# A hand-written order for every engine in a kernel of windowed attention followed by a feed-forward network

## The chip, the cores and the metric

One core of one Trainium2 chip runs the whole program. The metric is the device time of one execution in microseconds (us). A core has a matmul engine (PE, with weight loads listed as PEld), a vector engine (DVE), an activation engine (ACT), a GpSimd engine (POOL in the profile) and SP, which here only starts transfers. Matmul results are kept in accumulation banks (PSUM); both kernels use eight, each 128 partitions by 512 float32. Each engine works through its own list of instructions in order; engines wait for each other by semaphores.

## The reference, cut to what matters

```python
# attention: B, H, Sl, Sg, D = 8, 8, 512, 32, 64; window 32
s_g = scale * q_g @ k_all.T            # 32 global queries see all 544 keys
s_l = concat(scale * q_l @ k_g.T,      # 512 local queries see the 32 global keys
             where(|i-j| <= 32, scale * q_l @ k_l.T, -1e9))
out = concat(softmax(s_g) @ v_all, softmax(s_l) @ v_all)
# feed-forward on all 4352 tokens of width 512, hidden width 2048
h = x @ w_in
out = (h * sigmoid(1.702 * h)) @ w_out
```

## The kernel before

Matmuls use bf16 operands. Four heads make a "quad"; a batch is two quads, called a and c below. The feed-forward part is cut into steps `k`: 16 steps per batch of 512 tokens. Step `k` does one slice of the hidden layer (`h_step`: four matmuls of 512 columns on PE, tanh on ACT, the gate multiply on DVE) and, 24 steps later, a quarter of one output tile (`o_step`: four matmuls). Attention for batch `i+1` is a generator whose pieces are handed out between the steps of batch `i`. A tile scheduler then sets the order on each engine.

```python
# (cut) PSUM: 4 banks for scores, 1 for value products, 2 for hp, 1 for op
psS = ...(name="psS", bufs=4); psV = ...(bufs=1); psH = ...(bufs=2); psO = ...(bufs=1)

def load_v(Q):
    ...                                   # transfer of the values into st, float32
    if Q < 4:
        nc.scalar.activation(v[:, :, : 4 * D], st, AF.Copy)
    else:
        nc.gpsimd.tensor_copy(v[:, :, : 4 * D], st)

def quad(Q):                              # (cut)
    # DVE: two transposes of 128x1024 (kT, qT)
    # twice: scores on 4 banks (PE), 4 exponentials (ACT), one mask multiply (DVE); yield
    # row sums, then value products h=0 and h=1, all through the one psV bank; yield after each
    #   row sums:      DVE transpose sT, reciprocal, transpose back (rs)
    #   value product: DVE multiply xL = ov * rs frees the bank
    # global queries: og through the same bank; DVE reciprocal, ACT four scaled copies (xg),
    #   DVE transpose into xG; yield

def h_step(i, fc):
    ...                                   # four matmuls into hp
    nc.scalar.activation(th, hp, AF.Tanh, scale=0.851)
    nc.vector.scalar_tensor_tensor(gT, in0=th, scalar=1.0, in1=hp, op0=ALU.add, op1=ALU.mult)

def batch(b):
    if b == 1:
        transpose_g(4, NQ)
    if 1 <= b < B - 1:
        expand_g(b + 1, nc.gpsimd)        # four multiplies: block-diagonal global k, q, v
    a, c = quad(2 * b), quad(2 * b + 1)
    for g in (a, a, c, a, c, a, a, a, c, c, c, c):
        yield next(g, None)

LAG = 24
for _ in batch(0):
    pass
for k in range(NBK * FC + LAG):           # (cut)
    # h_step(k), o_step(k - 24), then pieces of batch(i + 1), 12 per 16 steps
```

The softmax here doesn't subtract the row's maximum and nothing guards it: scores larger than these inputs give would overflow.

## Time and profile before

| | before |
|---|---|
| time, median | 389.0 us |
| PE busy | 347.3 us (89%) |
| one steady period: 16 steps and one batch of attention | 37.9 us, PE busy 37.7 |
| feed-forward steps finished by 167 us | about 48 of 168 |

First the page of the kernel before: busy time by engine, and the span in 40 slices (each digit is the busy share of a slice in tenths; PEclk is the granted PE clock in tenths).

```profile
span 389.2 us, 7403 instructions
...
PE 347.3 (89%) x2960; PEld 178.4 (46%) x2960; DVE 223.8 (58%) x362; ACT 188.3 (48%) x375; POOL 135.8 (35%) x205
...
PE   0396777999999979999999999999999999999984
...
PEclk9999999899699998999999999999999999999999
DMA  9999999119992685936713000000101100111112
```

PE is full from about slice 15 on (counted from 0). Before that it shares the time with transfers and waits. The windows view of the same kernel (busy microseconds of each engine in a stretch, then granted clock and transfer share) tells the stages apart:

```profile
13.50:60.00 46.50, 34.58 (x272) 18.44 (x272) 21.35 (x36) 18.44 (x36) 32.69 (x59) 1.00 1.25 170
60.00:100.00 40.00, 36.74 (x365) 19.59 (x363) 31.85 (x47) 21.54 (x44) 24.31 (x35) 0.95 0.89 98
...
204.60:242.50 37.90, 37.74 (x360) 19.47 (x359) 25.35 (x39) 21.82 (x45) 2.08 (x2) 1.00 0.14 43
...
318.00:389.00 71.00, 63.43 (x319) 30.92 (x317) 18.44 (x33) 23.06 (x46) 0.00 (x0) 1.00 0.14 49
```

The third line is one steady period. PE (the first pair) is busy in 37.74 of 37.90 us, DVE in 25.35 and ACT in 21.82. So in the steady stage PE is the limit and has nothing to give away: any wait put on PE there is paid in full. One caution: the clock record of this run begins at its first switch, at 47.9 us. Until then the 1.00 of the view and the 9 of the page are no reading; 512-column matmuls start 0.43 us apart there and 0.216 us apart afterwards, so PE ran at half clock.

Two excerpts of the timeline of the kernel before, the first on DVE and the second on POOL (columns: start, duration, engine, line, operation, output and inputs, shapes, count):

```profile
141.37 4.54 DVE L259 TENSOR_TENSOR e_1884<-e_1884,mask 128x1408 bf16<-128x1408 bf16 x1
```

```profile
140.69 1.16 POOL L162 TENSOR_TENSOR kgBD_170<-kgT,bdm 128x512 bf16<-128x512 bf16 x1
141.81 1.15 POOL L162 TENSOR_TENSOR qgBD_171<-qgT,bdm 128x512 bf16<-128x512 bf16 x1
142.91 1.14 POOL L162 TENSOR_TENSOR vgU_172<-rvg,bdm 128x512 bf16<-128x512 bf16 x1
144.02 1.14 POOL L162 TENSOR_TENSOR vgBD_173<-rvg,bdm 128x512 bf16<-128x512 bf16 x1
```

Of the 32 mask multiplies of this kernel 26 take 0.84 to 0.89 us, and five take 1.13 to 1.76 us, each beside work on GpSimd. This one took 4.54 us: it began during the first of GpSimd's four multiplies and ended 0.75 us after the last of them.

### The profile page before, as it was taken

Reading aid. Unit: us, or ns where it says so; the run is one execution under the profiler, and the core shown is the slowest. Engines: PE = TensorE matmul, PEld = TensorE weight load, DVE = VectorE, ACT = ScalarE, POOL = GpSimd, SP = SyncE. Lnnn points to the kernel's source line nnn. Section 1 sums busy time; section 2 is a strip of 40 time slices with the busy share of each in tenths; the row PEclk is TensorE's granted clock in tenths of the full one; section 3 lists DMA queues with packets and bytes.
Section 4 is the critical chain, followed back from the end, with each engine's and each line's share of the span. In section 5 each row is a group of like instructions: output and inputs, shape, how many; then the busy total and the mean of one; then the engine's idle time right before and its main releaser. Section 6 shows DMA issues by size and latency. Waiting matters only on the chain.

```text
span 389.2 us, 7403 instructions
## 1 busy us (share of the span) xinstructions
PE 347.3 (89%) x2960; PEld 178.4 (46%) x2960; DVE 223.8 (58%) x362; ACT 188.3 (48%) x375; POOL 135.8 (35%) x205
## 2 busy tenths in 40 slices
PE   0396777999999979999999999999999999999984
PEld 0253433544544434555555555555455544455531
DVE  4434359776797794658656855685545644333200
ACT  2462236625556843386448544854485443434311
POOL 8857937277890995826530011000000000000000
PEclk9999999899699998999999999999999999999999
DMA  9999999119992685936713000000101100111112
GB/s 155 190 189 179 112 185 145 12 34 175 172 106 59 104 116 57 135 83 83 112 51 83 29 28 29 29 29 28 49 7 38 45 29 27 40 43 54 53 57 54
DMA packets 83314, 31.15 MB, mean 80 GB/s; under 512 B 75856, under 2 KB 77904, under 8 KB 83280
## 3 DMA queue, kind: packets, MB, share of 16 engines
q0 software_dynamic: 44496, 13.38, 32.7%
q1 hardware_dynamic: 38784, 17.31, 18.3%
q8 instruction: 23, 0.38, 0.4%
q14 instruction: 11, 0.09, 0.1%
HBM read 35.13 MB, written 8.91 MB: 113 GB/s over the span
## 4 chain that ended last, share of the span: by engine, by line
PE 62%; DMA 11%; POOL 8%; ACT 8%; issue 6%; DVE 5%; ACTq 0%; DVEq 0%; POOLq 0%
PE op L337 26%; PE hp L322 21%; PE s L231 4%; DMA w_in_sb<-in_moe_w_in_dram 4%; PE ov L280 4%; PE s L253 4%; POOL rk L77 3%; POOL rq L77 3%; DMA rk<-in_k_l_dram 2%; DMA rq<-in_q_l_dram 2%; PE ov L273 2%; DMA w_out_sb<-in_moe_w_out_dram 2%; ACT ob L341 2%; ACT xg L305 2%; ACT th L325 2%
## 5 line engine op out<-in xcount | busy, mean ns | idle before, releaser
L322 PE MATMUL hp<-xL,w_in_sb 128*128 128x512 bf16 x512 | 136.9, 391 | 9.8 <-DVE gT L326 9.7
L337 PE MATMUL op<-w_out_sb,gT 128*128 128x512 bf16 x544 | 138.5, 381 | 3.7 <-ACT ob L341 2.8
L325 ACT ACTIVATE th<-hp 128x512 f32<-128x512 f32 (+1 forms) x144 | 83.0, 579 | 113.2 <-PE hp L322 111.2
L326 DVE SCALAR_TENSOR_TENSOR gT<-th,hp 128x512 bf16<-128x512 f32 (+1 forms) x144 | 93.4, 652 | 66.7 <-ACT th L325 66.1
L337 PEld LDWEIGHTS <-gT 128*128 128x128 bf16 x544 | 53.1, 98 | 67.5 <-issue 9.3
L322 PEld LDWEIGHTS <-w_in_sb 128*128 128x128 bf16 x576 | 53.3, 99 | 66.0 <-issue 16.9
L231 PE MATMUL s<-qT,kT 32*128 32x160 bf16 (+1 forms) x512 | 29.6, 252 | 16.8 <-DVE qT L216 14.2
L77 POOL DMA_DIRECT2D rk<-in_k_l_dram x64 | 37.2, 589 | 16.0 <-DVE kT L216 7.3
L77 POOL DMA_DIRECT2D rq<-in_q_l_dram x64 | 36.6, 577 | 8.2 <-DMA rq<-in_q_l_dram 3.0
L305 ACT ACTIVATE xg<-og,rg 32x64 bf16<-32x64 f32 x64 | 19.5, 305 | 30.2 <-DVE rg L301 29.6
L231 PEld LDWEIGHTS <-kT 32*128 32x128 bf16 x512 | 16.2, 96 | 33.5 <-issue 20.8
L341 ACT ACTIVATE ob<-op 128x512 f32<-128x512 f32 x34 | 20.5, 603 | 21.9 <-PE op L337 21.9
L293 DVE TENSOR_TENSOR xL<-ov,rs 128x512 bf16<-128x512 f32 x32 | 21.9, 686 | 8.3 <-PE ov L280 8.1
L216 DVE STREAM_TRANSPOSE kT<-rk 128x1024 bf16<-128x1024 bf16 x16 | 21.1, 1320 | 6.4 <-DMA rk<-in_k_l_dram 5.4
L216 DVE STREAM_TRANSPOSE qT<-rq 128x1024 bf16<-128x1024 bf16 x16 | 20.7, 1296 | 4.9 <-DMA rq<-in_q_l_dram 4.9
L287 DVE STREAM_TRANSPOSE sT<-ov 128x512 f32<-128x512 f32 x16 | 11.4, 711 | 7.6 <-PE ov L280 7.6
L306 DVE STREAM_TRANSPOSE xG<-xg 128x64 bf16<-128x64 bf16 x16 | 3.9, 246 | 19.8 <-ACT xg L305 19.8
L91 POOL CAST v_89<-vst 128x1024 bf16<-128x1024 f32 x3 | 3.1, 1040 | 28.3 <-issue 28.3
L291 DVE STREAM_TRANSPOSE rs<-rT 128x512 f32<-128x512 f32 x16 | 11.3, 708 | 0.5
L253 PEld LDWEIGHTS <-kT 128*128 128x128 bf16 x128 | 8.0, 100 | 7.6 <-issue 4.9
L186 POOL DMA_DIRECT2D w_in_sb<-in_moe_w_in_dram x16 | 8.5, 533 | 4.8 <-DMA w_in_sb<-in_moe_w_in_dram 4.3
L322 PE MATMUL hp<-xG,w_in_sb 128*128 128x256 bf16 x64 | 9.8, 273 | 0.1
(364 smaller groups left out, 347.9 us busy)
## 6 DMA issues: line engine op xcount, KB each, us to landing
vst<-in_v_l_dram SPq DMA_DIRECT2D x64, 128.0 KB, 4.6
out_dram<-ob SPq DMA_DIRECT2D x32, 256.0 KB, 2.0
rk<-in_k_l_dram POOLq DMA_DIRECT2D x64, 64.0 KB, 3.2
rq<-in_q_l_dram POOLq DMA_DIRECT2D x64, 64.0 KB, 3.7
w_in_sb<-in_moe_w_in_dram POOLq DMA_DIRECT2D x16, 128.0 KB, 7.1
w_out_sb<-in_moe_w_out_dram POOLq DMA_DIRECT2D x4, 512.0 KB, 9.2
out_dram<-ob SPq DMA_DIRECT2D x8, 64.0 KB, 1.7
rkg<-in_k_g_dram POOLq DMA_DIRECT2D x1, 192.0 KB, 12.6
```

Of the source, the lines that this page charges most:

```text
L77: nc.gpsimd.dma_start(out=r[32 * j : 32 * j + 32], in_=src[Q, j])
L216: nc.vector.transpose(dst.rearrange("p h (n r t) -> p h n t r", n=8, t=2), src.rearrange("p n (t h d) -> p h n t d", t=2, h=2),)
L231: nc.tensor.matmul(ps[j][:, col : col + wd], lhsT=kT[p, h, 128 * c : 128 * c + 128], rhs=qT[p, h, q0 : q0 + wd], start=(h == 0), stop=(h = ...
L253: nc.tensor.matmul(o, lhsT=l(h), rhs=r(h), start=(h == 0), stop=(h == 1), skip_group_check=True)
L280: nc.tensor.matmul(ov[32 * j : 32 * j + 32, q0 : q0 + wd], lhsT=lv, rhs=E[c // 2][:, j, col : col + wd], start=False, stop=(c == 3), skip_ ...
L293: nc.vector.tensor_mul(x[:, 2 * u + h, :], ov, rs)
L305: nc.scalar.activation(xg[p, :], og[p, j * D : (j + 1) * D], AF.Copy, scale=rg[p, j : j + 1])
L322: nc.tensor.matmul(hp[:, :n], lhsT=w_in_sb[:, kc, fc * 128 : (fc + 1) * 128], rhs=(xL[i] if i < B else xG)[:, kc, :], start=(kc == 0), sto ...
L325: nc.scalar.activation(th[:, :n], hp[:, :n], AF.Tanh, scale=0.851)
L326: nc.vector.scalar_tensor_tensor(gTs[i][:, fc, :n], in0=th[:, :n], scalar=1.0, in1=hp[:, :n], op0=ALU.add, op1=ALU.mult)
L337: nc.tensor.matmul(ops[i], lhsT=gTs[i][:, fc, tci * 128 : tci * 128 + 128], rhs=w_out_sb[:, fc, :], start=(fc == 0), stop=(fc == FC - 1))
L341: nc.scalar.activation(ob, ops[i], AF.Copy, scale=0.5)
```

## The change

Its intent: no scheduler, and no elementwise work on GpSimd. The order on each engine is the order of the program. The first batch's attention uses all eight banks. Feed-forward of batch 0 then runs alone on three banks, attention of batch 1 runs alone, and from then on a table of 16 rows gives each feed-forward step its pieces of attention. Inside a step PE does `h`, then attention, then `o`; ACT does half of the exponentials, tanh, then the rest; DVE does the gate multiply, then attention. The casts of the values go to ACT, the expansions of the global keys, queries and values to DVE.

```diff
+    ctx.enter_context(tc.manual_schedule())
...
-        if Q < 4:
-            nc.scalar.activation(v[:, :, : 4 * D], st, AF.Copy)
-        else:
-            nc.gpsimd.tensor_copy(v[:, :, : 4 * D], st)
+        nc.scalar.activation(v[:, :, : 4 * D], vst.pop(Q), AF.Copy)
...
-            eng.tensor_mul(
+            nc.vector.tensor_mul(
...  (the generator quad() becomes a class: T transposes, S scores, X exponentials, M mask,
...   U(0) row sums, U(1), U(2) value products, R1/R2 their reciprocals, XL(h) the multiplies,
...   Gm global product, G1 reciprocal, G2 scaled copies, G3 transpose)
+    def step(k, pe=(), act0=(), act1=(), dve=()):   # cut: guards for the last steps
+        h_mm(k)
+        for f in pe: f()
+        o_mm(k - LAG)
+        for f in act0: f()
+        h_tanh(k)
+        for f in act1: f()
+        h_mul(k)
+        o_out(k - LAG)
+        for f in dve: f()
...
+        V(0, lambda: c.T(0))
+        soft(a, 0, 0); soft(a, 1, 2)      # S in row r, X and M in row r+1
+        V(2, lambda: c.T(1))
+        soft(c, 0, 4)
+        P(5, lambda: a.U(0));  V(5, lambda: a.R1())
+        soft(c, 1, 6)
+        V(6, lambda: a.R2())
+        P(7, lambda: a.U(1));  V(8, lambda: a.XL(0))
+        P(9, lambda: a.U(2));  V(9, lambda: a.XL(1))
+        P(10, lambda: a.Gm()); V(10, lambda: a.G1())
+        A1(11, lambda: a.G2()); V(11, lambda: a.G3())
+        P(11, lambda: c.U(0)); V(11, lambda: c.R1())
+        V(12, lambda: c.R2())
+        P(12, lambda: c.U(1)); V(13, lambda: c.XL(0))
+        P(13, lambda: c.U(2)); V(13, lambda: c.XL(1))
+        P(14, lambda: c.Gm()); V(14, lambda: c.G1())
+        A1(15, lambda: c.G2()); V(15, lambda: c.G3())
+            V(4, lambda: transpose_g(2 * n, 2 * n + 2))     # next batch n
+            V(4, lambda: expand_g(n, (0,)))
+            V(7, lambda: expand_g(n, (1, 2)))
+            V(10, lambda: expand_g(n, (3,)))
+            A1(8, lambda: cast_v(2 * n)); A1(13, lambda: cast_v(2 * n + 1))
+            V(14, lambda: quads(n)[0].T(0)); V(15, lambda: quads(n)[0].T(1))
...
+    for k in range(FC):
+        step(k)                            # feed-forward of batch 0 alone
...  (attention of batch 1 alone, rows of the same table in order)
+    for k in range(FC, (B + 1) * FC + LAG):
+        step(k, **(row k % FC of att_table(k // FC + 1)))
```

More of the change, by code (lines that the diff above doesn't have):

```diff
@@ L81, with cast_v @@
     vtiles = []
+    vst = {}
     def load_v(Q):
-        st = ld.tile([128, 4, 4 * D], F32, name="vst", bufs=2)
+        vst[Q] = ld.tile([128, 4, 4 * D], F32, name="vst", bufs=2)
         for j in range(4):
-            nc.sync.dma_start(out=st[:, :, j * D : (j + 1) * D], in_=vf[Q, j])
+            nc.sync.dma_start(out=vst[Q][:, :, j * D : (j + 1) * D], in_=vf[Q, j])
+    def cast_v(Q):
         v = vtiles[Q % 4]
-        if Q < 4:
-            nc.scalar.activation(v[:, :, : 4 * D], st, AF.Copy)
-        else:
-            nc.gpsimd.tensor_copy(v[:, :, : 4 * D], st)
+        nc.scalar.activation(v[:, :, : 4 * D], vst.pop(Q), AF.Copy)
         loaded[Q][2] = v
@@ L156, in transpose_g, with expand_g @@
             )
-    def expand_g(b, eng):
+    def expand_g(b, which=(0, 1, 2, 3)):
         qs = slice(2 * b, 2 * b + 2)
         def bd(dst, src, n, w):
-            eng.tensor_mul(
+            nc.vector.tensor_mul(
                 dst.rearrange("p n (j w) -> p n j w", j=4),
@@ L169, in expand_g @@
         m = lambda t: t.rearrange("p a h c -> p (a h) c")
-        bd(m(kgBD), m(kgT[:, qs]), 4, 32)
-        bd(m(qgBD), m(qgT[:, qs]), 4, 32)
-        bd(m(vgU), rvg[:, qs, :].rearrange("p a (h d) -> p (a h) d", h=2), 4, 32)
-        bd(vgBD[:, :, : 4 * D], rvg[:, qs, :], 2, D)
-    transpose_g(0, 2)
-    expand_g(0, nc.vector)
+        todo = (
+            (m(kgBD), m(kgT[:, qs]), 4, 32),
+            (m(qgBD), m(qgT[:, qs]), 4, 32),
+            (m(vgU), rvg[:, qs, :].rearrange("p a (h d) -> p (a h) d", h=2), 4, 32),
+            (vgBD[:, :, : 4 * D], rvg[:, qs, :], 2, D),
+        )
+        for i in which:
+            bd(*todo[i])
     w_in_sb = wts.tile([128, NKC, d_ff], BF16)
@@ L197 @@
     load_g(4, NQ)
-    transpose_g(2, 4)
-    expand_g(1, nc.vector)
     xG = consts.tile([128, NKC, B * Sg], BF16)
@@ L204, with __init__, T @@
     WIN = ((0, 160), (96, 192), (224, 192), (352, 160))
-    def quad(Q):
-        b, u = divmod(Q, 2)
-        rk, rq, v = loaded[Q]
-        kgBD, qgBD, vgU, vgBD = GB[b % 3]
-        if u == 0:
-            xL[b] = att.tile([128, NKC, Sl], BF16, name="xL", bufs=3)
-        x = xL[b]
-        kT = att.tile([128, 2, Sl], BF16, name="kT")
-        qT = att.tile([128, 2, Sl], BF16, name="qT")
-        for dst, src in ((kT, rk), (qT, rq)):
+    class Quad:
+        def __init__(self, Q):
+            self.Q = Q
+            self.b, self.u = divmod(Q, 2)
+            if self.u == 0:
+                xL[self.b] = att.tile([128, NKC, Sl], BF16, name="xL", bufs=3)
+            self.x = xL[self.b]
+            self.G = GB[self.b % 3]
+            self.E = []
+            self.ps = None
+            self.st = {}
+        def T(self, i):
+            rk, rq, _ = loaded[self.Q]
+            src = (rk, rq)[i]
+            dst = att.tile([128, 2, Sl], BF16, name=("kT", "qT")[i])
             nc.vector.transpose(
@@ L219, in quad, with S @@
             )
-        if Q + 4 < NQ:
-            load(Q + 4)
-        E = []
-        for rnd in range(2):
-            ps = [psS.tile([128, 512], F32, name="s") for _ in range(4)]
+            self.st["kq"[i]] = dst
+        def S(self, rnd, alt=False):
+            kT, qT = self.st["k"], self.st["q"]
+            kgBD, qgBD, vgU, vgBD = self.G
+            u = self.u
+            if alt:
+                ps = [psH.tile([128, 512], F32, name="s2", tag="hp") for _ in range(2)]
+                ps.append(psO.tile([128, 512], F32, name="s2", tag="op"))
+                ps.append(psV.tile([128, 512], F32, name="s2", tag="ov"))
+            else:
+                ps = [psS.tile([128, 512], F32, name="s") for _ in range(4)]
             col = 0
@@ L240, in quad @@
                 c = 2 * rnd + i
-                full.append((ps[i][:, LW : LW + 128], lambda h, c=c: kT[:, h, 128 * c : 128 * c + 128],
+                full.append((ps[i][:, LW : LW + 128],
+                             lambda h, c=c: kT[:, h, 128 * c : 128 * c + 128],
                              lambda h: qgBD[:, u, h, :]))
@@ L254, in quad, with X, M @@
                                      skip_group_check=True)
-            e = att.tile([128, 4, 512], BF16, name="e%d" % rnd)
-            for j in range(4):
+            self.ps = ps
+            self.E.append(att.tile([128, 4, 512], BF16, name="e%d" % rnd))
+        def X(self, *js):
+            e = self.E[-1]
+            for j in js:
                 n = 480 if j < 2 else 512
-                nc.scalar.activation(e[:, j, :n], ps[j][:, :n], AF.Exp, scale=scale)
+                nc.scalar.activation(e[:, j, :n], self.ps[j][:, :n], AF.Exp, scale=scale)
+        def M(self, rnd):
+            e = self.E[rnd]
             nc.vector.tensor_mul(
@@ L262, in quad, with U @@
             )
-            E.append(e)
-            yield
-        pieces = ((E[0][:, 3, LW:512], 0, 160), (E[1][:, 2, LW:512], 160, 160),
-                  (E[1][:, 3, LW:512], 320, 160), (E[0][:, 2, 480:512], 480, 32))
-        rs = None
-        for unit in range(3):
-            ov = psV.tile([128, 512], F32, name="ov")
+        def U(self, unit, pool=None, tag="ov"):
+            E, v = self.E, loaded[self.Q][2]
+            vgU = self.G[2]
+            ov = (pool or psV).tile([128, 512], F32, name="ov", tag=tag)
             h = unit - 1
-            lg = onesBD if unit == 0 else vgU[:, u, h, :]
+            lg = onesBD if unit == 0 else vgU[:, self.u, h, :]
+            pieces = ((E[0][:, 3, LW:512], 0, 160), (E[1][:, 2, LW:512], 160, 160),
+                      (E[1][:, 3, LW:512], 320, 160), (E[0][:, 2, 480:512], 480, 32))
             for i, (e, q0, wd) in enumerate(pieces):
@@ L284, in quad @@
                     )
-            if unit == 0:
-                sT = att.tile([128, 16, 32], F32, name="sT")
-                nc.vector.transpose(sT.rearrange("p a b -> p (a b)"), ov)
-                rT = att.tile([128, 16, 1], F32, name="rT")
-                nc.vector.reciprocal(rT, sT[:, :, 0:1])
-                rs = att.tile([128, 512], F32, name="rs")
-                nc.vector.transpose(rs.rearrange("p (a b) -> p a b", a=16), rT.to_broadcast([128, 16, 32]))
-            else:
-                nc.vector.tensor_mul(x[:, 2 * u + h, :], ov, rs)
@@ L294, in quad @@
-            yield
-        og = psV.tile([128, 4 * D + 4], F32, name="og", tag="ov")
-        for c in range(4):
-            nc.tensor.matmul(og, lhsT=E[c // 2][:, c % 2, LW : LW + 128], rhs=v[:, c, :],
-                             start=(c == 0), stop=False)
-        nc.tensor.matmul(og, lhsT=E[0][:, 2, LW : LW + 128], rhs=vgBD[:, u, :], start=False, stop=True)
-        rg = att.tile([128, 4], F32, name="rg")
-        nc.vector.reciprocal(rg, og[:, 4 * D :])
-        xg = att.tile([128, D], BF16, name="xg")
@@ L303, in quad @@
-        for j in range(4):
-            p = slice(32 * j, 32 * j + 32)
-            nc.scalar.activation(xg[p, :], og[p, j * D : (j + 1) * D], AF.Copy, scale=rg[p, j : j + 1])
-        nc.vector.transpose(xG[:, 2 * u : 2 * u + 2, Sg * b : Sg * b + Sg],
-                            xg.rearrange("p (h d) -> p h d", h=2))
-        if Q + 4 < NQ:
-            load_v(Q + 4)
-        yield
-    NBK = (n_tokens + TB - 1) // TB
-    gTs = {}
-    ops = {}
-    def h_step(i, fc):
+            self.st[unit] = ov
@@ new lines, in R1, with R2 @@
+        def R1(self):
+            sT = att.tile([128, 16, 32], F32, name="sT")
+            nc.vector.transpose(sT.rearrange("p a b -> p (a b)"), self.st[0])
+            rT = att.tile([128, 16, 1], F32, name="rT")
+            nc.vector.reciprocal(rT, sT[:, :, 0:1])
+            self.st["rT"] = rT
+        def R2(self):
+            rs = att.tile([128, 512], F32, name="rs")
+            nc.vector.transpose(rs.rearrange("p (a b) -> p a b", a=16),
+                                self.st["rT"].to_broadcast([128, 16, 32]))
+            self.st["rs"] = rs
@@ new lines, in XL, with Gm @@
+        def XL(self, h):
+            nc.vector.tensor_mul(self.x[:, 2 * self.u + h, :], self.st[1 + h], self.st["rs"])
+        def Gm(self, pool=None, tag="ov"):
+            E, v = self.E, loaded[self.Q][2]
+            og = (pool or psV).tile([128, 4 * D + 4], F32, name="og", tag=tag)
+            for c in range(4):
+                nc.tensor.matmul(og, lhsT=E[c // 2][:, c % 2, LW : LW + 128], rhs=v[:, c, :],
+                                 start=(c == 0), stop=False)
+            nc.tensor.matmul(og, lhsT=E[0][:, 2, LW : LW + 128], rhs=self.G[3][:, self.u, :],
+                             start=False, stop=True)
+            self.st["og"] = og
@@ new lines, in G1, with G2 @@
+        def G1(self):
+            rg = att.tile([128, 4], F32, name="rg")
+            nc.vector.reciprocal(rg, self.st["og"][:, 4 * D :])
+            self.st["rg"] = rg
+        def G2(self):
+            og, rg = self.st["og"], self.st["rg"]
+            xg = att.tile([128, D], BF16, name="xg")
+            for j in range(4):
+                p = slice(32 * j, 32 * j + 32)
+                nc.scalar.activation(xg[p, :], og[p, j * D : (j + 1) * D], AF.Copy,
+                                     scale=rg[p, j : j + 1])
+            self.st["xg"] = xg
@@ L317, in h_step, with G3, h_mm @@
+        def G3(self):
+            nc.vector.transpose(
+                xG[:, 2 * self.u : 2 * self.u + 2, Sg * self.b : Sg * self.b + Sg],
+                self.st["xg"].rearrange("p (h d) -> p h d", h=2))
+    gTs, ops, hps, ths = {}, {}, {}, {}
+    LAG = 24
+    def h_mm(k):
+        i, fc = divmod(k, FC)
         n = TB if i < B else B * Sg
@@ L319, in h_step, with h_tanh, h_mul, o_mm @@
             gTs[i] = moe.tile([128, FC, TB], BF16, name="gT", bufs=3)
-        hp = psH.tile([128, TB], F32, name="hp")
+        if k < LAG - 2 and k % 3 == 2:
+            hp = psO.tile([128, TB], F32, name="hp", tag="op")
+        else:
+            hp = psH.tile([128, TB], F32, name="hp", tag="hp")
         for kc in range(NKC):
             nc.tensor.matmul(hp[:, :n], lhsT=w_in_sb[:, kc, fc * 128 : (fc + 1) * 128],
-                             rhs=(xL[i] if i < B else xG)[:, kc, :], start=(kc == 0), stop=(kc == NKC - 1))
-        th = moe.tile([128, TB], F32, name="th")
-        nc.scalar.activation(th[:, :n], hp[:, :n], AF.Tanh, scale=0.851)
-        nc.vector.scalar_tensor_tensor(gTs[i][:, fc, :n], in0=th[:, :n], scalar=1.0, in1=hp[:, :n],
-                                       op0=ALU.add, op1=ALU.mult)
-    def o_step(i, st):
+                             rhs=(xL[i] if i < B else xG)[:, kc, :],
+                             start=(kc == 0), stop=(kc == NKC - 1))
+        hps[k] = hp
+    def h_tanh(k):
+        n = TB if k // FC < B else B * Sg
+        th = moe.tile([128, TB], F32, name="th")
+        nc.scalar.activation(th[:, :n], hps[k][:, :n], AF.Tanh, scale=0.851)
+        ths[k] = th
+    def h_mul(k):
+        i, fc = divmod(k, FC)
+        n = TB if i < B else B * Sg
+        nc.vector.scalar_tensor_tensor(gTs[i][:, fc, :n], in0=ths.pop(k)[:, :n], scalar=1.0,
+                                       in1=hps.pop(k)[:, :n], op0=ALU.add, op1=ALU.mult)
+    def o_mm(k):
+        i, st = divmod(k, FC)
         n = TB if i < B else B * Sg
@@ L334, in o_step @@
         if f4 == 0:
-            ops[i] = psO.tile([128, d_model], F32, name="op")
+            ops[i] = psO.tile([128, d_model], F32, name="op", tag="op")
         for fc in range(4 * f4, 4 * f4 + 4):
@@ L338, in o_step @@
                              rhs=w_out_sb[:, fc, :], start=(fc == 0), stop=(fc == FC - 1))
-        if f4 == 3:
-            ob = moe.tile([128, d_model], F32, name="ob")
-            nc.scalar.activation(ob, ops[i], AF.Copy, scale=0.5)
-            if i < B:
-                r = i * S + Sg + tci * 128
-                nc.sync.dma_start(out=out[r : r + 128, :], in_=ob)
-            else:
-                for j in range(4):
-                    r = (4 * tci + j) * S
-                    nc.sync.dma_start(out=out[r : r + Sg, :], in_=ob[32 * j : 32 * j + 32, :])
@@ L350, in batch, with o_out @@
-    def batch(b):
-        if b == 1:
-            transpose_g(4, NQ)
-        if 1 <= b < B - 1:
-            expand_g(b + 1, nc.gpsimd)
-        a, c = quad(2 * b), quad(2 * b + 1)
-        for g in (a, a, c, a, c, a, a, a, c, c, c, c):
-            yield next(g, None)
-    LAG = 24
-    NP = 12
-    for _ in batch(0):
-        pass
-    g = iter(())
-    for k in range(NBK * FC + LAG):
-        i, st = divmod(k, FC)
-        if st == 0:
-            g = batch(i + 1) if i + 1 < B else iter(())
-            done = 0
-        if i < NBK:
-            h_step(i, st)
-        if 0 <= k - LAG < NBK * FC:
-            o_step(*divmod(k - LAG, FC))
-        while done * FC < (st + 1) * NP and done < NP:
-            next(g, None)
-            done += 1
+    def o_out(k):
+        i, st = divmod(k, FC)
+        n = TB if i < B else B * Sg
+        tci, f4 = divmod(st, 4)
+        if tci * 128 >= n or f4 != 3:
+            return
+        ob = moe.tile([128, d_model], F32, name="ob")
+        nc.scalar.activation(ob, ops[i], AF.Copy, scale=0.5)
+        if i < B:
+            r = i * S + Sg + tci * 128
+            nc.sync.dma_start(out=out[r : r + 128, :], in_=ob)
+        else:
+            for j in range(4):
+                r = (4 * tci + j) * S
+                nc.sync.dma_start(out=out[r : r + Sg, :], in_=ob[32 * j : 32 * j + 32, :])
@@ new lines @@
+    a, c = Quad(0), Quad(1)
+    a.T(0), a.T(1)
+    transpose_g(0, 2)
+    expand_g(0)
+    a.S(0)
+    a.X(0, 1, 2, 3)
+    a.M(0)
+    cast_v(0)
+    a.S(1, alt=True)
+    c.T(0), c.T(1)
+    a.X(0, 1, 2, 3)
+    a.M(1)
+    c.S(0)
+    cast_v(1)
+    c.X(0, 1, 2, 3)
+    a.U(0)
+    a.R1(), a.R2()
+    a.U(1, psO, "op")
+    a.XL(0)
+    c.M(0)
+    a.U(2, psH, "hp")
+    a.XL(1)
+    c.S(1)
+    a.Gm(psH, "hp")
+    a.G1()
+    c.X(0, 1, 2, 3)
+    a.G2()
+    c.M(1)
+    a.G3()
+    c.U(0)
@@ new lines @@
+    c.R1(), c.R2()
+    c.U(1, psO, "op")
+    c.XL(0)
+    c.U(2, psH, "hp")
+    c.XL(1)
+    c.Gm(psH, "hp")
+    c.G1(), c.G2(), c.G3()
+    def step(k, pe=(), act0=(), act1=(), dve=()):
+        if k < (B + 1) * FC:
+            h_mm(k)
+        for f in pe:
+            f()
+        if k >= LAG:
+            o_mm(k - LAG)
+        for f in act0:
+            f()
+        if k < (B + 1) * FC:
+            h_tanh(k)
+        for f in act1:
+            f()
+        if k < (B + 1) * FC:
+            h_mul(k)
+        if k >= LAG:
+            o_out(k - LAG)
+        for f in dve:
+            f()
@@ new lines, with quads, att_table, soft @@
+    NQD = {}
+    def quads(b):
+        if b not in NQD:
+            NQD[b] = (Quad(2 * b), Quad(2 * b + 1)) if b < B else None
+        return NQD[b]
+    def att_table(b):
+        a, c = quads(b)
+        L = [dict(pe=[], act0=[], act1=[], dve=[]) for _ in range(FC)]
+        P = lambda s, f: L[s]["pe"].append(f)
+        A0 = lambda s, f: L[s]["act0"].append(f)
+        A1 = lambda s, f: L[s]["act1"].append(f)
+        V = lambda s, f: L[s]["dve"].append(f)
+        def soft(q, r, s):
+            P(s, lambda: q.S(r))
+            A0(s + 1, lambda: q.X(0, 1))
+            A1(s + 1, lambda: q.X(2, 3))
+            V(s + 1, lambda: q.M(r))
+        V(0, lambda: c.T(0))
+        soft(a, 0, 0)
+        soft(a, 1, 2)
+        V(2, lambda: c.T(1))
+        soft(c, 0, 4)
+        P(5, lambda: a.U(0))
+        V(5, lambda: a.R1())
+        soft(c, 1, 6)
+        V(6, lambda: a.R2())
+        P(7, lambda: a.U(1))
+        V(8, lambda: a.XL(0))
+        P(9, lambda: a.U(2))
+        V(9, lambda: a.XL(1))
+        P(10, lambda: a.Gm())
+        V(10, lambda: a.G1())
+        A1(11, lambda: a.G2())
+        V(11, lambda: a.G3())
+        P(11, lambda: c.U(0))
+        V(11, lambda: c.R1())
+        V(12, lambda: c.R2())
+        P(12, lambda: c.U(1))
+        V(13, lambda: c.XL(0))
+        P(13, lambda: c.U(2))
+        V(13, lambda: c.XL(1))
+        P(14, lambda: c.Gm())
+        V(14, lambda: c.G1())
+        A1(15, lambda: c.G2())
+        V(15, lambda: c.G3())
+        if b + 1 < B:
+            n = b + 1
+            L[0]["pe"].insert(0, lambda: (load_v(2 * n), load_v(2 * n + 1)))
+            V(4, lambda: transpose_g(2 * n, 2 * n + 2))
+            V(4, lambda: expand_g(n, (0,)))
+            V(7, lambda: expand_g(n, (1, 2)))
+            V(10, lambda: expand_g(n, (3,)))
+            A1(8, lambda: cast_v(2 * n))
+            A1(13, lambda: cast_v(2 * n + 1))
+            V(14, lambda: quads(n)[0].T(0))
+            V(15, lambda: quads(n)[0].T(1))
+        if b + 2 < B:
+            L[4]["pe"].insert(0, lambda: (load(2 * b + 4), load(2 * b + 5)))
+        return L
@@ new lines @@
+    load(4), load(5)
+    for k in range(FC):
+        step(k)
+    q1 = quads(1)
+    q1[0].T(0), q1[0].T(1)
+    transpose_g(2, 4)
+    expand_g(1)
+    cast_v(2)
+    cast_v(3)
+    a, c = q1
+    L1 = att_table(1)
+    for s in range(FC):
+        for f in L1[s]["pe"] + L1[s]["act0"] + L1[s]["act1"]:
+            f()
+        for f in L1[s]["dve"]:
+            f()
+    for k in range(FC, (B + 1) * FC + LAG):
+        b = k // FC + 1
+        if k % FC == 0 and b < B:
+            L = att_table(b)
+        step(k, **(L[k % FC] if b < B else {}))
```

## The prediction

> **What bounds it now.** The page shows PE busy 89%, DVE 58%, ACT 48%, POOL 35%. By windows there are three stages. (a) To 167 us: only 48 of 168 feed-forward steps are done. PE starts at 13.6 us; in the timeline 512-column matmuls follow each other at 0.43 us until 47 us (half speed), at 0.216 us afterwards. The Trainium skill, "TensorE: Matmul & The Clock Gate", section "What's actually happening", has those two states and a window of about 3.4 us; the trace agrees on the states. (b) 167 to 318 us: a 16-step period with one batch of attention takes 37.85 us, PE busy 37.6 of it: 32 groups of four matmuls at 0.865 us, plus 10.2 us of attention. No slack. (c) 318 to 389 us: no attention; 71 us.
>
> **What the change moves.** The work on PE is the same; the old order let the scheduler fill gaps, the new is fixed.
> - Start: batch 0's scores use all eight banks, and the second round runs four row groups at once. But transfers (rq of quad 1 read at 20.6 us) and half clock remain. I estimate the first feed-forward step at 37.5 us, then 16 steps on three buffers at 0.87 us instead of 1.21: done near 53 us (before: about 66).
> - Batch 1's attention then runs alone. Its chain (transposes 1.3 each, four rounds of exponentials 2.0 each, value products through one bank) takes about 27 us for 10 us of PE work, plus about 5 because PE likely falls to half clock. Step 16 starts near 85 us; the start's gain is gone.
> - GpSimd loses casts (1.04 us each) and expansions (1.15). ACT gets the casts (1.06, 2 per period), DVE the expansions (0.45, 4 per period): about 27.5 us of DVE and 24 of ACT per period, neither the bound.
>
> **The main cost: stalls built into the table.** Per period PE waits in order (durations from the trace):
> 1. Step 9: a's third value product waits for a multiply behind the mask multiply and two expansions on DVE: about 0.8 us.
> 2. Step 11: c's row sum needs the bank that a's scaled copies free, which ACT runs after that step's tanh: 1.04+0.60+1.26 after the matmul's start, less 0.87: about 2.1 us.
> 3. Step 13: c's third product needs the bank freed by a DVE multiply behind the same step's gate multiply: 1.04+0.60+0.65+0.69 less 0.87: about 2.2 us.
> 4. Step 0 of the next batch: scores need the second transpose, placed on DVE behind ACT's scaled copies of step 15: about 1.85 us.
> So a period should be about 44.5 us, for six periods (the first about 42, with half the output steps). All is on the critical path.
>
> **Sum.** 85 + 42 + 5 x 44.5 - 2 + 71 = 418, say 417 us; 8 in 10 within 403 to 429. Faster by over 2%: 0.05; within 2%: 0.06; slower by over 2%: 0.89.
>
> **What would show it.** Windows of a period: PE busy about 37.8 of 44.5 us. Waits: row sums on ACT's scaled copies, value products on the DVE multiply, scores on the DVE transpose; each about 2 us, some six times. Timeline: feed-forward begins at 37 to 38 us; 16 steps by 53; then 27 to 33 us with PE under half busy; step 16 at 80 to 87 us. The tail is 71 us as before.
>
> **What would make it wrong.** If the lone batch takes 20 us, or the waits overlap other work, the time nears 400. If transfers or half clock hold the start longer, or slow DVE instructions like one 4.5 us mask multiply recur, it exceeds 425.

## The result, and the profile after

The changed kernel takes 424.35 us (median of four runs, 421.14 to 426.71), the kernel before 389.0. The ratio is 1.093, with a 95% interval of 1.082 to 1.103: slower. A ratio here is the mean time of one kernel's runs over the mean of the other's runs of the same rounds, so it is not quite the ratio of the medians.

The page of the changed kernel:

```profile
span 422.8 us, 7348 instructions
...
PE 335.5 (79%) x2915; PEld 176.1 (42%) x2960; DVE 227.1 (54%) x396; ACT 200.4 (47%) x387; POOL 95.8 (23%) x169
...
PE   0488572578888978899689968998699789999984
...
PEclk9999955599989998999999998999999899999999
DMA  9799999993009400880069001400001000110122
```

The row of PE has a hole in slices 5 to 7 (counted from 0), where the clock is halved, and afterwards it never holds nine for long. (The trace of this run lacks 45 of 2960 matmul records, so its PE time is a little too low.) The windows of the changed kernel, to be read against those of before:

```profile
13.00:47.20 34.20, 27.88 (x292) 15.92 (x293) 24.09 (x41) 21.35 (x42) 27.15 (x50) 1.00 1.02 137
47.20:85.00 37.80, 18.51 (x230) 12.42 (x232) 19.30 (x35) 13.78 (x25) 21.11 (x35) 0.57 1.42 172
...
217.93:263.21 45.28, 39.00 (x352) 20.00 (x358) 27.01 (x45) 23.88 (x46) 6.86 (x12) 0.96 0.43 69
...
352.00:423.00 71.00, 62.00 (x309) 30.51 (x313) 17.72 (x32) 21.84 (x43) 0.00 (x0) 0.99 0.14 49
```

The third line is one steady period. It took 45.28 us, where before had 37.90, with the same work; DVE and ACT are far from full. Row 0 of the table begins at 128.94, 174.27, 217.93, 263.21 and 306.86 us, so periods of about 45.3 and 43.65 us alternate here. The tail is as before. The waits view of the changed kernel names who waits for whom (total us, times, longest):

```profile
PE s L245 <- DVE qT L223: 29.3, 9, 13.0
...
PE ov L295 <- DVE xL L323: 17.2, 14, 2.0
PE ov L295 <- ACT xg L345: 12.7, 7, 2.0
...
PE ov L295 <- DVE sT L311: 7.8, 2, 7.0
```

The first line holds three waits of the start (13.0 us the longest) and then one per period, 9.5 us in all. In the kernel before the largest sum of PE waits outside the start was 9.7 us, for the gate multiply. The timeline of PE in the changed kernel shows the three large waits of one period (in brackets: idle before, and what ended it):

```profile
215.28 1.03 PE L367 MATMUL hp<-xL,w_in_sb 128*128 128x512 bf16 x4
217.93 0.48 PE L245 MATMUL s<-qT,kT 32*128 32x160 bf16 x16 [1.63 <-DVE qT L223]
...
243.34 1.03 PE L367 MATMUL hp<-xL,w_in_sb 128*128 128x512 bf16 x4
246.20 0.23 PE L295 MATMUL ov<-e_2933,onesBD 128*128 128x160 bf16 x1 [1.83 <-ACT xg L345]
...
250.28 1.03 PE L367 MATMUL hp<-xL,w_in_sb 128*128 128x512 bf16 x4
253.31 0.23 PE L295 MATMUL ov<-e_2933,vgU_172 128*128 128x160 bf16 x1 [2.01 <-DVE xL L323]
...
254.34 1.89 PE L393 MATMUL op<-w_out_sb,gT 128*128 128x512 bf16 x4
256.02 1.55 PE L367 MATMUL hp<-xL,w_in_sb 128*128 128x512 bf16 x4
257.41 0.39 PE L329 MATMUL og<-v_93,e_2933 128*128 128x260 bf16 x2
```

The last lines show an extra price. After the third wait, four matmuls that take 1.03 us together took 1.89: the granted clock of PE was at half from 253.66 to 257.07 us, 3.4 us. Such a dip lies in the first, second, fourth and sixth of the six periods, each time within 1.6 us of the end of a wait of 1.8 to 2.0 us. It accounts for the difference between 43.65 and 45.28 us: 3.4 us at half clock lose about 1.7.

How a wait is built can be read from the other engines in the same stretch. ACT runs the tanh of step 11 and only then the scaled copies that free the bank; DVE runs the gate multiply of step 13 and only then the multiply that frees it:

```profile
244.41 0.60 ACT L375 ACTIVATE th<-hp 128x512 f32<-128x512 f32 x1 [1.69 <-PE hp L367]
244.90 1.25 ACT L345 ACTIVATE xg<-og,rg 32x64 bf16<-32x64 f32 x4
```

```profile
251.97 0.69 DVE L381 SCALAR_TENSOR_TENSOR gT<-th,hp 128x512 bf16<-128x512 f32 x1 [1.10 <-ACT th L375]
252.58 0.68 DVE L323 TENSOR_TENSOR xL<-ov,rs 128x512 bf16<-128x512 f32 x1
```

Both chains begin with a matmul of the same step: PE issues `h`, then stands before a bank which is freed only behind the tanh of that very `h`. The value to be multiplied or copied had been ready a step earlier.

Finally the lone attention of batch 1. On DVE of the changed kernel:

```profile
57.32 0.89 DVE L281 TENSOR_TENSOR e_802<-e_802,mask 128x1408 bf16<-128x1408 bf16 x1 [1.04 <-ACT e_802 L277]
64.65 0.31 DVE L155 STREAM_TRANSPOSE kgT<-rkg 128x128 bf16<-128x128 bf16 x1 [6.44 <-DMA rkg<-in_k_g_dram]
67.19 0.31 DVE L155 STREAM_TRANSPOSE qgT<-rqg 128x128 bf16<-128x128 bf16 x1 [2.23 <-DMA rqg<-in_q_g_dram]
```

DVE stands still for the global keys of batch 2 (one transfer brings those of all later batches), whose transfer lies behind the second weight; PE waits 6.97 us behind it (the 7.0 in the last line of the waits).

### The profile page after: what moved, and what is told of

Read it like the earlier page. It is cut to its first block, busy times and chain, and to the rows that moved or that the text cites. A ratio compares the mean times of both kernels' runs of the same rounds, so it can differ in the third digit from the quotient of the medians.

```text
span 422.8 us, 7348 instructions
## 1 busy us (share of the span) xinstructions
PE 335.5 (79%) x2915; PEld 176.1 (42%) x2960; DVE 227.1 (54%) x396; ACT 200.4 (47%) x387; POOL 95.8 (23%) x169
## 4 chain that ended last, share of the span: by engine, by line
PE 60%; DMA 10%; POOL 8%; ACT 8%; issue 6%; DVE 6%; DVEq 0%; POOLq 0%; ACTq 0%
PE op L393 26%; PE hp L367 21%; DMA rvg<-in_v_g_dram 5%; PE s L268 4%; DMA w_in_sb<-in_moe_w_in_dram 3%; ACT xg L345 3%; PE ov L302 3%; POOL rq L78 3%; POOL rk L78 3%; PE s L245 2%; PE ov L295 2%; DMA rq<-in_q_l_dram 2%; DVE xL L323 2%; DVE qT L223 2%; ACT th L375 1%
## 5 line engine op out<-in xcount | busy, mean ns | idle before, releaser
L393 PE MATMUL op<-w_out_sb,gT 128*128 128x512 bf16 x508 | 136.0, 386 | 7.7 <-ACT ob L403 4.7
L367 PE MATMUL hp<-xL,w_in_sb 128*128 128x512 bf16 x503 | 131.3, 387 | 2.1 <-DVE xL L323 1.1
L367 PEld LDWEIGHTS <-w_in_sb 128*128 128x128 bf16 x576 | 57.1, 100 | 67.5 <-issue 6.5
L393 PEld LDWEIGHTS <-gT 128*128 128x128 bf16 x544 | 50.2, 98 | 58.1 <-issue 9.2
L245 PE MATMUL s<-qT,kT 32*128 32x160 bf16 (+1 forms) x496 | 19.2, 253 | 31.4 <-DVE qT L223 29.3
L245 PEld LDWEIGHTS <-kT 32*128 32x128 bf16 x512 | 11.3, 98 | 45.6 <-issue 22.8
L295 PEld LDWEIGHTS <-onesBD 128*128 128x128 bf16 x64 | 6.0, 106 | 18.0 <-issue 15.1
L295 PEld LDWEIGHTS <-vgU_164 128*128 128x128 bf16 x48 | 4.6, 108 | 18.5 <-issue 17.2
```

The source lines that it names most:

```text
L245: nc.tensor.matmul(ps[j][:, col : col + wd], lhsT=kT[p, h, 128 * c : 128 * c + 128], rhs=qT[p, h, q0 : q0 + wd], start=(h == 0), stop=(h = ...
L295: nc.tensor.matmul(ov[:, q0 : q0 + wd], lhsT=lg, rhs=e, start=(i == 0), stop=False, skip_group_check=True)
L367: nc.tensor.matmul(hp[:, :n], lhsT=w_in_sb[:, kc, fc * 128 : (fc + 1) * 128], rhs=(xL[i] if i < B else xG)[:, kc, :], start=(kc == 0), sto ...
L393: nc.tensor.matmul(ops[i], lhsT=gTs[i][:, fc, tci * 128 : tci * 128 + 128], rhs=w_out_sb[:, fc, :], start=(fc == 0), stop=(fc == FC - 1))
```

## The experiments

My theory: the loss is the waits that the table itself builds in, three of about 2 us and one small one per period, six periods. Rival 1: the loss is the work moved from GpSimd onto ACT and DVE. Rival 2: the loss is at the start, where batch 1 runs alone. Each experiment was timed in three rounds beside the kernel before. They ran on three chips (e1 to e4; e5, e6, e8, e9 and e12; e10 and e11), where the kernel before had medians of 388.9 to 390.6 us; a difference below 2 us between two medians of different chips shows nothing.

| run | what | median us | ratio to before | 95% interval |
|---|---|---|---|---|
| (changed kernel) | | 424.35 | 1.093 | 1.082 to 1.103 |
| e1_bank | global product of a on a score bank | 413.36 | 1.064 | 1.059 to 1.070 |
| e2_xl | c's first multiply one row earlier | 411.48 | 1.058 | 1.053 to 1.063 |
| e3_tr | next batch's transposes earlier | 414.45 | 1.063 | 1.058 to 1.069 |
| e4_all | all three, and one more bank | 380.45 | 0.976 | 0.972 to 0.981 |
| e5_pool | only: elementwise work back on GpSimd | 428.98 | 1.099 | 1.092 to 1.107 |
| e6_kg | only: lone batch, global keys later | 417.22 | 1.067 | 1.060 to 1.075 |
| e8_start | e4 and a new start | 368.74 | 0.944 | 0.938 to 0.949 |
| e9_allpool | e4 with elementwise work on GpSimd | 389.85 | 0.998 | 0.991 to 1.005 |
| e10_bnopool | before, elementwise work off GpSimd | 389.17 | 1.000 | 0.995 to 1.006 |
| e11_fourbanks | changed, first batch on four banks | 423.31 | 1.087 | 1.079 to 1.095 |
| e12_spare | e4 and spare GpSimd multiplies | 385.0 | 0.988 | 0.982 to 0.995 |

All gave correct results.

**e1_bank: the wait of step 11 alone.**

```diff
-        P(10, lambda: a.Gm())
+        P(10, lambda: a.Gm(psS, "s"))
```

> One edit: a's global product takes a bank of the score pool (idle at steps 8 to 15) instead of the single value bank, so c's row sum at step 11 no longer waits for ACT's scaled copies. Table-stall theory: the waits of row sums on the scaled copies (about 1.85 us each, 12.7 us in all, the one in the lone batch included) go, each of the six periods shortens by about 1.8 us, 11 us in all: about 413 us, 1.062 of before. Rival (the work moved from GpSimd to ACT and DVE is the cost) and rival (the loss is at the start): no change beyond 2 us, because the stall would only move to the next wait.

Measured: 413.36 us, 11.0 less than the changed kernel's median. The waits for the scaled copies are gone from its list of waits. Periods are 42.05 us, and 43.7 with a half-clock dip. A period without a dip is thus 1.6 us shorter and not 1.83, because a wait of 0.23 us for DVE's transpose of the row sums takes its place; the lone batch gives another 1.4 us. As the table-stall theory said; the rivals said no change.

**e2_xl: the wait of step 13 alone.**

```diff
         V(12, lambda: c.R2())
+        V(12, lambda: c.XL(0))
-        V(13, lambda: c.XL(0))
```

> One edit: c's first value multiply moves on DVE from behind the gate multiply of step 13 to the end of step 12, same work, same banks. Table-stall theory: the 2.0 us wait of c's third product in each of six periods goes, and so does the half-clock stretch that follows some of them: 12 to 14 us, about 411 us, 1.056 of before. Rivals (moved work, start): no change beyond 2 us.

Measured: 411.48 us, 12.9 less. The same instruction, a few places earlier on its engine. Not all of it is the wait: a period without a dip falls from 43.65 to 42.06 us, 1.6 us and not 2.01, because a wait of 0.41 us stays. The rest is dips: one is left of the four in the periods (the start came 1.1 us later).

**e3_tr: the wait of step 0 alone.**

```diff
-            V(14, lambda: quads(n)[0].T(0))
-            V(15, lambda: quads(n)[0].T(1))
+            V(10, lambda: quads(n)[0].T(0))
+            V(14, lambda: quads(n)[0].T(1))
```

> One edit: the two big transposes of the next batch's first quad move from steps 14 and 15 to steps 10 and 14 on DVE. Table-stall theory: the 1.6 us wait of the scores of step 0 goes in each of the six periods, 9 to 10 us: about 414.5 us, 1.066 of before. Rivals: no change beyond 2 us.

Measured: 414.45 us, 9.9 less. The wait is gone; a period without a dip takes 41.97 us, and all four dips remain.

**e4_all: all of it.** The three edits, and for the small wait of step 9:

```diff
-        P(9, lambda: a.U(2))
+        P(9, lambda: a.U(2, psS, "s"))
```

> The three edits together, and a's third product of step 9 on a bank of the score pool as well. Table-stall theory: the savings add up, a period falls from about 45.2 to about 38 us with PE busy over 37, and the six periods give back about 40 us: about 385 us, 0.99 of before. Rival (moved work): the period stays above 42 us as ACT or DVE become the next wait, over 405 us. Rival (start is the loss): the time stays above 410 us.

Measured: 380.45 us, 43.9 less than the changed kernel and 2.4% faster than the kernel before (interval 1.9 to 2.8%). One period in the windows of e4_all:

```profile
156.21:194.10 37.89, 37.64 (x359) 19.45 (x358) 26.97 (x44) 23.74 (x47) 9.06 (x17) 1.00 0.52 85
```

PE is busy in 37.64 of 37.89 us, as in the kernel before, and from 87 us on no half clock is left. A period without a dip has become 5.76 us shorter (43.65 to 37.89), and the four waits seen in the changed kernel add up to just that: 1.83 + 2.01 + 1.63 + 0.28 = 5.75. In six periods these are at most 34.6 us; the rest of the 43.9 lies in the dips, about 1.7 us each, and in the start (row 0 begins at 84.18 us instead of 87.90). This settles that the table's waits were the main loss. The start of this kernel still has the lone batch, so rival 2 cannot have been the main loss against before; e6 shows what part it had.

**e5_pool: the elementwise work back on GpSimd, table untouched.**

```diff
-        nc.scalar.activation(v[:, :, : 4 * D], vst.pop(Q), AF.Copy)
+        if Q < 4:
+            nc.scalar.activation(v[:, :, : 4 * D], vst.pop(Q), AF.Copy)
+        else:
+            nc.gpsimd.tensor_copy(v[:, :, : 4 * D], vst.pop(Q))
...
-            nc.vector.tensor_mul(
+            (nc.vector if b < 2 else nc.gpsimd).tensor_mul(
```

> The changed kernel with its table untouched, but the elementwise work given back to GpSimd: the casts of the values from the third batch on (off ACT) and the expansions of the global keys, queries and values from the third batch on (off DVE). Rival theory (the moved work is the cost): most of the 35 us comes back, under 405 us. Table-stall theory: the three 2 us waits of a period stand behind tanh, scaled copies, gate multiply and transposes, which all stay where they are, so 421 to 426 us as the changed kernel; at most the small wait of step 9, behind two expansions, shrinks (2 us in all).

Measured: 428.98 us, 4.6 more by the medians. Rival 1 falls: putting the work back gains nothing. My range of 421 to 426 was missed. The intervals of the two ratios overlap (1.082 to 1.103 and 1.092 to 1.107), so this run alone does not show that the work back on GpSimd costs time; e9, on the mended table, does.

**e6_kg: the lone batch without its wait for the late transfer.**

```diff
-            V(4, lambda: transpose_g(2 * n, 2 * n + 2))
-            V(4, lambda: expand_g(n, (0,)))
-            V(7, lambda: expand_g(n, (1, 2)))
-            V(10, lambda: expand_g(n, (3,)))
+            t, x = (10, 10) if b == 1 else (4, 7)
+            V(t, lambda: transpose_g(2 * n, 2 * n + 2))
+            V(t, lambda: expand_g(n, (0,)))
+            V(x, lambda: expand_g(n, (1, 2)))
+            V(max(x, 10), lambda: expand_g(n, (3,)))
```

> One edit in the lone attention of batch 1: the transposes and expansions of the next batch's global keys move from rows 4, 7 and 10 of the table to row 10, so that DVE no longer stands waiting for the late global-key transfer (6.4 and 2.2 us) in front of the row-sum transposes that PE waits for (7.0 us). Start theory in this narrow form: step 16 starts about 7 us earlier (78 instead of 85 us) and all of it reaches the end: about 417 us, 1.072 of before. If the transfers bound the start anyway, step 16 moves by less than 2 us and the time stays at 424.

Measured: 417.22 us, 7.1 less. Step 16 begins at 76.76 us instead of 85.03. So the wait for the global keys was real and reached the end.

**e8_start: a better start on the mended table.** On top of e4: steps 0 to 7 of batch 0 alone, steps 8 to 15 each followed by two rows of batch 1's attention; global keys and the next quads loaded before the second weight; in batch 1 the next batch's global work in row 12 and its transposes in rows 14 and 15; c's third product on a score bank too.

```diff
-    for k in range(FC):
-        step(k)
+    for k in range(8):
+        step(k)
...
-    for s in range(FC):
-        for f in L1[s]["pe"] + L1[s]["act0"] + L1[s]["act1"]:
-            f()
-        for f in L1[s]["dve"]:
-            f()
+    for s in range(8):
+        step(8 + s, **L1[2 * s])
+        for key in ("pe", "act0", "act1", "dve"):
+            for f in L1[2 * s + 1][key]:
+                f()
```

> A candidate to beat both: all the mends of the table, and the start redone: eight feed-forward steps of batch 0 alone, then the other eight between the rows of batch 1's attention, two rows per step; global keys and queries of later batches loaded ahead of the second weight. If the lone batch costs its latency chain and not transfers, step 16 starts near 68 us instead of 84, and the rest follows as in the mended table: about 366 us, 0.94 of before. If transfers bound the start, step 16 stays above 78 us and the time above 375 us.

Measured: 368.74 us, 5.6% faster than the kernel before. Step 16 begins at 66.8 us. This version beats both kernels. It holds several edits at once, so the share of each is not known.

**e9_allpool: the mended table with the elementwise work on GpSimd.** The edits of e4 and e5 together.

> The mended table (all four edits) with the elementwise work given back to GpSimd as in the run before. With the stalls gone PE has no slack, so if taking the work off GpSimd is worth anything it must show here. Theory (PE-bound period, ACT and DVE at two thirds): same as the mended table within 2 us, about 380 us. Rival (GpSimd work was holding DVE back, or ACT and DVE are now the tighter queues): a difference of more than 4 us in either direction.

Measured: 389.85 us, 9.4 more than e4_all. I had expected no difference: a miss, and the more useful one. The steady period is 37.92 us, just as in e4_all; the loss lies in the first period, which took 44.5 us instead of 34.1. In the timeline of e9_allpool, first DVE, then POOL:

```profile
102.98 7.02 DVE L284 TENSOR_TENSOR e<-e,mask 128x1408 bf16<-128x1408 bf16 x1
```

```profile
102.82 1.17 POOL L167 TENSOR_TENSOR kgBD<-kgT,bdm 128x512 bf16<-128x512 bf16 x1
103.94 1.15 POOL L167 TENSOR_TENSOR qgBD<-qgT,bdm 128x512 bf16<-128x512 bf16 x1
105.05 1.15 POOL L167 TENSOR_TENSOR vgU<-rvg,bdm 128x512 bf16<-128x512 bf16 x1
106.14 1.03 POOL L96 CAST v<-vst 128x1024 bf16<-128x1024 f32 x1
107.14 1.14 POOL L167 TENSOR_TENSOR vgBD<-rvg,bdm 128x512 bf16<-128x512 bf16 x1
108.23 1.03 POOL L96 CAST v<-vst 128x1024 bf16<-128x1024 f32 x1
```

One mask multiply took 7.02 us instead of 0.89: it began during the first of six GpSimd instructions in a row and ended 0.74 us after the last. PE stood 4.4 us behind it. The same picture is in e5_pool (7.16 us) and in the kernel before (4.54 us, above). But it is the exception. Four other mask multiplies of e9_allpool met the same row of instructions and took 1.59 us, and then GpSimd's next instruction was the one that was stretched, here from 1.03 to 1.70 us:

```profile
141.04 1.59 DVE L284 TENSOR_TENSOR e<-e,mask 128x1408 bf16<-128x1408 bf16 x1 [0.29 <-ACT e L280]
```

```profile
140.73 1.16 POOL L167 TENSOR_TENSOR vgU<-rvg,bdm 128x512 bf16<-128x512 bf16 x1
141.82 1.70 POOL L96 CAST v<-vst 128x1024 bf16<-128x1024 f32 x1
```

The Trainium skill, "SBUF — State Buffer", section "Who interferes with whom", says that DVE and GpSimd share one pair of ports, as an exclusive lock, and that a DVE instruction with two inputs from that memory is among those that block. The trace agrees: the mask multiply has two such inputs, and the multiplies with one input from an accumulation bank stayed below 0.70 us in this run. A second part of the loss is another 3.9 us wait of PE: the expansions stood in GpSimd's queue behind the issue of transfers.

**e12_spare: the contention by itself.** The mended table with 12 GpSimd multiplies on scratch tiles after each batch's transfers; nothing waits for them by data.

```diff
+    def spare():
+        for _ in range(12):
+            nc.gpsimd.tensor_mul(scr[2], scr[0], scr[1])
...
-            L[4]["pe"].insert(0, lambda: (load(2 * b + 4), load(2 * b + 5)))
+            L[4]["pe"].insert(0, lambda: (load(2 * b + 4), load(2 * b + 5), spare()))
```

> The mended table, where GpSimd does no elementwise work, with twelve idle-handed GpSimd multiplies (128x512 bf16, about 1.15 us each, on scratch tiles that nothing else touches) added after each batch's key and query transfers, in five batches (60 in all). No instruction of another engine waits for them by data. Contention theory (a two-input DVE multiply stands still while GpSimd's multiplies run): some of the mask multiplies take several us instead of 0.89, the gate multiplies, which read one input from the accumulation banks, stay at 0.65 to 0.69, and the time rises by 5 to 30 us over 380.5. Rival (in the run with GpSimd work only its data or its place in the transfer queue cost time): every mask multiply stays at 0.85 to 0.9 us and the time within 3 us of 380.5.

Measured: 385.0 us, about 4.5 more than e4_all. In its timeline, DVE:

```profile
164.33 2.75 DVE L284 TENSOR_TENSOR e<-e,mask 128x1408 bf16<-128x1408 bf16 x1 [0.29 <-ACT e L280]
```

Eleven mask multiplies took 1.24 to 2.75 us, ten of them beside a spare multiply; in e4_all none of the 32 took over 0.9 us, though 14 ran while GpSimd issued transfers. The gate multiplies and the multiplies by the reciprocals (one input from an accumulation bank) stayed below 0.70 us. So GpSimd's work alone, without any data between them, stretches DVE's two-input multiplies. None stood through a whole row here. In e12 each spare multiply waits on a semaphore for the one before it, but so do the four in the kernel before, behind which a mask multiply stood for 4.54 us; what decides between one instruction and the whole row is not shown.

**e10_bnopool: this part of the change alone, in the kernel before.**

```diff
-        if Q < 4:
-            nc.scalar.activation(v[:, :, : 4 * D], st, AF.Copy)
-        else:
-            nc.gpsimd.tensor_copy(v[:, :, : 4 * D], st)
+        nc.scalar.activation(v[:, :, : 4 * D], st, AF.Copy)
...
-            expand_g(b + 1, nc.gpsimd)
+            expand_g(b + 1, nc.vector)
```

> One part of the change alone, in the kernel before with its own scheduler: the casts of the values to ACT and the expansions to DVE, nothing else. If GpSimd's elementwise work stretches DVE's two-input multiplies (in the profile of before one mask multiply took 4.54 us where the others take 0.85 to 0.89, while four GpSimd expansions ran; the run with the mended table and GpSimd work had one of 7.02 us), these stretched ones go and the time falls by 3 to 8 us: 382 to 387 us. If the elementwise work is neutral: within 2 us of 389. If ACT or DVE become tight: slower.

Measured: 389.17 us, no change clear of the noise (ratio 0.995 to 1.006): a miss. All mask multiplies are now at 0.87 us on average, so the stretched ones are gone, yet the time did not fall by 3 us. The scheduler ordered everything anew. By 167 us the profiled run of e10 had done 50 hidden steps and 26 output steps, that of the kernel before 49 and 24, and its span is 387.3 us against 389.2. So a gain of up to about 2 us may be there, below what these runs can tell; where the rest went stays open.

**e11_fourbanks: the eight banks undone.**

```diff
-    a.S(1, alt=True)
+    a.S(1)
```

> The changed kernel with one part undone: batch 0's second score round waits for the four banks of the score pool instead of taking the other four. The transfer of the second quad's queries (its scores start at 20.0 us) hides it: the round would end near 19 us, before that. So no change within 2 us of the changed kernel, about 424 us. If the eight banks matter: 1 to 3 us slower.

Measured: 423.31 us, the same within the noise. The second quad's scores start at 20.2 us, against 19.98 with eight banks: they wait for its queries in both.

## Why the prediction was right

It said 417 us, within 403 to 429; 424.35 was measured. Its steps, one by one:

- **Steady stage without slack: right.** A period of before has PE busy in 37.74 of 37.90 us, and e4_all comes back to 37.89 once the waits are gone.
- **Four waits per period: right, each too large.** Predicted 2.1, 2.2, 1.85 and 0.8 us for steps 11, 13, 0 and 9. The trace shows 1.83, 2.01, 1.63 and, at step 9, 0.28. Taken away one by one, the first three shorten a period without a dip by 1.6, 1.6 and 1.7 us; all four together (e4) shorten it by 5.76 us, their whole sum. The 11.0, 12.9 and 9.9 us of the single runs hold dips and the lone batch too, and must not be divided by six.
- **The period of 44.5 us: right, by a cause that was missed.** The waits add up to 5.75 us, not 7. The half-clock dips after them, which I had not thought of, add 1.6 us to four of the six periods. The mean of 43.65 and 45.28 is 44.5; that two errors of opposite sign meet there is luck.
- **The start: the sum was right, its terms were not.** Step 16 was predicted near 85 us and began at 85.03. But the first feed-forward step came at 32.5 us, not 37.5: PE reached full clock near 25 us, where I had assumed half clock to the end. The 16 steps ended at 47.0 us instead of 53. The lone batch took 38.0 us instead of 32: a transfer that I had not followed made DVE, and PE behind it, stand for 7 us. Its half clock was foreseen (granted clock 0.57). That the errors cancel to 0.03 us is luck.
- **GpSimd's work neutral: wrong.** The prediction priced it only as busy time of ACT and DVE. On the mended table, leaving it on GpSimd costs 9.4 us (e9), 8 of them in two waits of PE, so there that part of the change is a gain. On the changed table itself e5 was 4.6 us slower by the medians, which its interval does not settle; in the scheduled kernel e10 shows no effect clear of the noise. A slow mask multiply was named as a danger of the new kernel; it belongs to the old one.
- **Where the missing 7 us are.** 424.35 is 7.35 us above 417. The six periods from step 16 took 264.6 us (85.03 to 349.60) where the prediction had 262.5, and what follows them 73.2 us where it had 71: 4.3 us in these two terms. Its terms sum to 418.5, of which it quoted 417: 1.5 us. The profile was read from the first to the last instruction, 422.8 us, 1.6 us less than the median that is compared: together 7.4 us. So the mis-sized terms are small, 2 us each.

## What to carry to other kernels

When the order is fixed by hand and the bottleneck engine has no slack, look for every place where that engine, after issuing work of a step, waits for a buffer that another engine frees only behind its own share of the same step: here two such places cost 24 us and transposes placed too late another 10 (the single edits e1 to e3, with the dips that they ended), and moving the instruction a row or more earlier, or taking an idle bank, removed them. Free a buffer as soon as its value is ready, ahead of the new step's work on that engine, and put transposes for the next stage several steps ahead of their use. Judge a bundle of changes by its parts: the same table with its waits mended is faster than before, and on that table taking elementwise work off GpSimd was worth 9 us, which the total hid.

## What the Trainium skill lacked or had wrong

- "TensorE: Matmul & The Clock Gate", section "What's actually happening", has the half clock return after an idle window of about 3.4 us. In the changed kernel PE fell to half clock for 3.4 us four times in the six periods, each time within 1.6 us of the end of a wait of 1.83 to 2.01 us; no PE gap in the 5 us before was longer. The same page's "A second HAM failure mode: psum-queue depth-cycling" does tell of short pauses that make the clock swing, but gives no length.
- The same page gives about 3.4 us of sustained work to reach full clock, in windows that run free of the program. The profiles agree with that: with one and the same program for the start, full clock came 3.4 to 3.7 us after PE's first matmul in e1, e2 and e6, and in the changed kernel only at 24.96 us, 5.0 us after PE had begun to work without a gap. What the page lacks is how full a window must be. In the kernel before, PE worked from 17.90 to 30.52 us with one gap of 0.17 us and stayed at half clock until 47.9 us (128-column matmuls start 0.107 us apart at 24.4 us, 512-column ones 0.43 us apart at 46 us); there the small matmuls of a score round went bank by bank instead of four row groups side by side. That this is the reason is not shown.
- "SBUF — State Buffer", section "Who interferes with whom", has the first to issue hold the ports for its whole instruction while the other blocks; it does not say who is next. Here a waiting DVE multiply mostly came in after one GpSimd instruction (1.59 us, four times in e9_allpool), but three times it stood through a whole row: six instructions (7.02 us in e9_allpool, 7.16 in e5_pool) and four (4.54 us in the kernel before).
